# Attention and gMLP on one core: transposes reordered in the first slots, the fifth slot without a group in its first hole, out weights loaded in the ninth slot

## The chip, the cores and the metric

The kernel runs on one core of a Trainium2 chip. The metric is the device time of one execution in microseconds (us), less is better. A core has a matrix engine (TensorE, PE in the profile; PEld is its loading of weights, which overlaps), a vector engine (DVE), a scalar engine (ACT), GpSimd (POOL) and SyncE (SP), which issues all data transfers here. The engines run beside each other, each takes its instructions in order, and semaphores hold an instruction until its inputs are there and its output's buffer is free.

## The reference

Eight batches, eight heads, 576 positions of 64 features. Attention is causal by blocks of 64 positions, and its output goes through a gated feed-forward layer with a product over positions. Cut to what matters:

```python
scores = np.matmul(q, k.transpose(0, 1, 3, 2)) / np.sqrt(D)
scores = np.where(block_i >= block_j, scores, -1e9)
attn = np.exp(scores - np.max(scores, axis=-1, keepdims=True))
attn = attn / (np.sum(attn, axis=-1, keepdims=True) + 1e-09)
x = np.matmul(attn, v)                      # heads side by side: 576 x 512 per batch
h = gelu(x @ w_in)                          # w_in 512 x 1024, tanh form of gelu
u, v = h[..., :512], h[..., 512:]
v_n = (v - mean(v)) / np.sqrt(var(v) + 1e-6) * g_ln
v_s = np.einsum('ts,bsd->btd', w_sg, v_n) + b_sg[None, :, None]
out = x + (u * v_s) @ w_out                 # w_out 512 x 512
```

The weights w_in and w_out arrive as 64-bit floats.

## The kernel before

**Slots.** The work is cut into 32 slots, slot(n) for n from 0 to 31: four pairs of heads for each of eight batches. "The first four slots" are 0 to 3, "the fifth" is slot 4, "the ninth" slot 8. Slot n finishes the attention of pair n (class Values) and makes the scores and exponents of pair n + 1 (class Scores). The names of its tiles are those of the profile:

- pa, pb, pc, pd: transposes of the probabilities. turn0 makes pa (key block 0), one tile per head, turn2 and turn2_rest pb (blocks 2 and 3), turn1 and turn1_rest pc (blocks 1 and 4), turn_first the start of pd. pd and pe later hold the transposed sums as well. Each tile is copied out to pt, for head a by ACT or DVE (table TE). These eight tiles of a slot go through three banks of the accumulator memory, so each waits until the copy of an earlier one, or what else reads it, has left the bank.
- s: the score products. step1 (tiles 4 and 1) and step2 (the rest of tile 4) stand together, step3 (tiles 3 and 0) and step4 (tile 2) later. DVE takes the maxima (negm), ACT the exponents (prob). s and all sums below share five banks.
- ob: attention times v, in av0, av2 and av1. x is the result, multiplied by the transposed reciprocal sums on DVE (x<-pe, x<-pd), and split into xh and xl for the feed-forward.

**Feed-forward of a batch.** It begins in the four slots behind the batch's own: 5 groups of matmuls for v (accv, the first of them the tail of 64 positions), 8 for u (accu), 8 for s (accs, the product over positions), and 8 for the output (acco) one batch later. A group is one step of a generator; hole(k) in a slot takes k groups, and a slot has seven holes, with the counts in PLAN, or in FIRST for slots 4 to 7. The groups of v, u and s of batch 0 lie in slots 4 to 7.

**The side queue.** gelu and the layer norm between v and s are not groups. v_part puts them into a queue, side, when its generator is taken up again behind its fifth group: gelu first (marked "G"), then moments (bs, stats), inverse_std (rs), centre (vv<-vv,stats,g_bc) and scale (vh, vl, vn_t, vone). run_side(k) takes up to k items but stops at a "G"; run_gelu takes a "G" and is called once in a slot, between the sixth and the seventh hole. s_part empties the queue when it begins. The first accs group then needs vh, vl, vn_t and vone.

**Weights.** load_weight loads and splits the weights step by step: from 64 bits (raw) through w to a high part (ACT) and a low part (POOL), with three instructions on DVE, two on ACT and one on POOL for each step, and AHEAD loads in flight. WS has the steps per slot, spread over four places in it; need(part) in the feed-forward takes the steps that are missing.

**Order.** TensorE's instructions keep the order of the program (keep_in_program_order). The order of DVE, ACT, POOL and SP is set when the program is built, by a scheduler that places instructions as they become ready in its model of time; on the chip each engine then runs that list in order. L88 and L91 in the profile are the helpers of matmul and transpose, L101 that of all other engines.

Of the kernel before, what the change touches and what calls it, by code (L numbers as in the profile page):

```python
# [28 lines left out]
def kernel(  # L29
# [13 lines left out]
    B, H, D, S = qT.shape  # L43
    P = 128
    BLK = 64
    DM = H * D
# [22 lines left out]
    def page(dtype, n, name):  # L69
        tag, bufs = KINDS.get(name, KINDS["w"])  # L70
        return sp.tile([P, n], dtype, tag=tag, name=name, bufs=bufs)

    def bank(tag, name, bufs):
        return psum.tile([P, 512], F32, tag=tag, name=name, bufs=bufs)

    def sbank(name):
        return bank("s", name, 5)

    def pbank(name):
        return bank("p", name, 3)  # L80
# [34 lines left out]
    def load_qk(n):  # L115
        b, h = PAIRS[n]
        if n == 0:

            q_f, k_f = page(F32, S, "w"), page(F32, S, "w")
        else:  # L120
            t = sp.tile([P, 2, S], F32, tag="qk_f", name="qk_f", bufs=1)
            q_f, k_f = t[:, 0, :], t[:, 1, :]
        SP.dma_start(q_f, qT[b, h : h + 2].rearrange("a d s -> (a d) s"))
        SP.dma_start(k_f, kT[b, h : h + 2].rearrange("a d s -> (a d) s"))
        qk[n] = (q_f, k_f) if n == 0 else t

    def split_qk(n):
        t = qk[n]
        hi = sp.tile([P, 2, S], F32R, tag="qk_h", name="qk_h", bufs=1)
        lo = sp.tile([P, 2, S], F32R, tag="qk_l", name="qk_l", bufs=1)  # L130
        V.tensor_copy(hi, t)
        for i in (1, 0):
            G.tensor_tensor(lo[:, i, :], t[:, i, :], hi[:, i, :].bitcast(F32), op=ALU.subtract)
        q_h, k_h, q_l, k_l = hi[:, 0, :], hi[:, 1, :], lo[:, 0, :], lo[:, 1, :]
        qk[n] = [(q_h, k_h), (q_h, k_l), (q_l, k_h)]

    def load_v(n):
        b, h = PAIRS[n]
        v_f = v_bufs[n % 2]
        cols = slice(h * D, (h + 2) * D)  # L140
        SP.dma_start(
            v_f[:, : NT - 1, :],
            v[b, : (NT - 1) * P, cols].rearrange("(j p) d -> p j d", p=P),
        )
        SP.dma_start(v_f[:TAIL, NT - 1, :], v[b, S - TAIL :, cols])
        vals[n] = v_f
# [6 lines left out]
    t = sbank("warm")  # L153
# [15 lines left out]
    for s in (0, 1):  # L169
        t = cp.tile([P, NT, 2 * D], F32, name=f"v_f{s}")  # L170
# [5 lines left out]
    for s in range(4):  # L176
        row = []
        for i in range(NT):
            t = cp.tile([P, P * (i + 1) if i else BLK], F32, name=f"prob{s}_{i}")
# [8 lines left out]
    wo_h = cp.tile([P, NC, DM], F32R, name="wo_h")  # L188
    wo_l = cp.tile([P, NC, DM], F32R, name="wo_l")
# [5 lines left out]
    def split_weight(x, dh, dl):  # L195
        A.copy(dh, x)
        G.tensor_tensor(dl, x, dh.bitcast(F32), op=ALU.subtract)

    def from_f64(raw, dh, dl):

        n = raw.shape[-1]
        words = raw.bitcast(U32).rearrange("p (n t) -> p n t", t=2)
        hi, lo = words[:, :, 1], words[:, :, 0]
        tm = page(U32, 2 * n, "w")
        t, m = tm[:, :n], tm[:, n:]

        A.mul(m.bitcast(F32), hi.bitcast(F32), 2.0**-112)

        V.tensor_scalar(t, lo, 29, None, op0=ALU.logical_shift_right)
        V.scalar_tensor_tensor(
            t, hi, 0x80000000, t, op0=ALU.bitwise_and, op1=ALU.bitwise_or
        )
        V.scalar_tensor_tensor(
            t, m, 3, t, op0=ALU.logical_shift_left, op1=ALU.bitwise_or
        )
        split_weight(t.bitcast(F32), dh, dl)

    def load_weight(src, cols, dh, dl):  # L220

        W, AHEAD = 256, 4
        parts = [(c, slice(f, f + W)) for f in range(cols.start, cols.stop, W) for c in range(NC)]
        raws = {}

        def fetch(k):
            if k < len(parts):
                c, fs = parts[k]
                raws[k] = page(src.dtype, W, "raw")
                SP.dma_start(raws[k], src[c * P : (c + 1) * P, fs])  # L230

        for k in range(AHEAD):
            fetch(k)
        for k, (c, fs) in enumerate(parts):
            args = (raws.pop(k), dh[:, c, fs], dl[:, c, fs])
            if src.dtype == F32:
                split_weight(*args)
            else:
                from_f64(*args)
            fetch(k + AHEAD)  # L240
            yield True

    def load_spatial():
        for j in range(NT - 1):
            t = page(F32, S, "w")
            SP.dma_start(t, w_sgT[j * P : (j + 1) * P, :])
            split_weight(t, ws_h[:, j, :], ws_l[:, j, :])
            yield True

        j = NT - 1  # L250
        t = page(F32, S, "w")
        for hf in (0, 1):
            SP.dma_start(t[hf * BLK : (hf + 1) * BLK, :], w_sgT[j * P : S, :])
        t2 = page(F32, S, "w")
        G.memset(t2[BLK:, :], 0.0)
        SP.dma_start(t2[BLK : BLK + 1, :], b_sg.unsqueeze(0))
        SP.dma_start(t2[96:97, :], b_sg.unsqueeze(0))
        A.copy(ws_h[:, j, :], t)
        G.tensor_tensor(
            ws_l[:BLK, j, :], t[:BLK, :], ws_h[:BLK, j, :].bitcast(F32), op=ALU.subtract  # L260
        )
        A.copy(ws_l[BLK:, j, :], t2[BLK:, :])
        V.tensor_tensor(
            ws_l[96:97, j, :], t2[96:97, :], ws_l[96:97, j, :].bitcast(F32), op=ALU.subtract
        )
        yield True

    def load_gains():
# [10 lines left out]
            ("u0", load_weight(w_in, slice(0, DH // 2), wi_h, wi_l)),  # L279
            ("u2", load_weight(w_in, slice(DH // 2, DH), wi_h, wi_l)),  # L280
            ("s", load_spatial()),
            ("o", load_weight(w_out, slice(0, DM), wo_h, wo_l)),
        ]
    )

    def weight_step():

        with ExitStack() as stack:
            for ins in newest.values():
                stack.enter_context(tc.issue_after(ins.ins))  # L290
            while weights and next(weights[0][1], None) is None:
                weights.popleft()
# [96 lines left out]
    class Values:  # L389
# [15 lines left out]
            pt = self.pt[a, j] = sp.tile([P, 512], F32, tag="pt", name="pt", bufs=4)  # L405
            copy(TE[a, j], pt, t)

        def turn0(self, a):

            t = pbank("pa")  # L410
            for i in (4, 3, 2, 1):
                self.turn(a, t[:, (i - 1) * P : i * P], i, 0)
            self.out(a, 0, t)

        def turn2(self):

# [99 lines left out]
    def run_side(k):  # L516

        while k > 0 and side and side[0][0] != "G":
            k -= 1
            side.popleft()[1]()  # L520
# [201 lines left out]
    def hole(k=1):  # L722

        while k > 0 and work:
            try:
                next(work[0])
                k -= 1
            except StopIteration:
                work.popleft()

    WS = [2, 2, 2, 1, 10, 3, 3, 3, 2]

    def load_share(n, k):

        if n < len(WS):
            for _ in range(WS[n] * (k + 1) // 4 - WS[n] * k // 4):
                weight_step()

    PLAN = ["1111111", "1111111", "1111111", "1111112"]

    FIRST = ["1111111", "1111101", "0011011", "1011010"]

    def slot(n, sc):
        va = Values(n, sc)
        nx = Scores(n + 1) if n + 1 < N else None
        g = [int(x) for x in (FIRST if n // 4 == 1 else PLAN)[n % 4]]
        if n + 2 < N:
            load_qk(n + 2)
        if n + 1 < N:
            load_v(n + 1)  # L750
        va.inverse()
        va.turn0(0)
        va.turn0(1)
        hole(g[0])
        load_share(n, 0)
        run_side(2)

        va.turn2()
        va.turn2_rest()
        if nx:  # L760
            nx.step1()
            nx.step2()
        va.av0()
        if nx:
            nx.exponents(1, 4)
        hole(g[1])
        load_share(n, 1)
        run_side(2)
        hole(g[2])
        run_side(2)  # L770
        va.turn1()
        va.turn1_rest()
        va.turn_first()
        if nx:
            nx.step3()
            nx.step4()
        va.av2()
        if nx:
            nx.exponents(3, 0, 2)
        hole(g[3])  # L780
        load_share(n, 2)
        run_side(2)
        va.av1()
        va.av00()
        va.turn_sums()
        hole(g[4])
        va.normalise()

        wait = n // (H // 2) > 0 and n % (H // 2) < 2
        pending.append(va.split)  # L790
        if not wait:
            while pending:
                pending.popleft()()
        run_side(2)
        if n + 2 < N:
            split_qk(n + 2)
        load_share(n, 3)
        hole(g[5])
        run_gelu()
        run_side(3)  # L800
        hole(g[6])
        run_side(3)
        if n % (H // 2) == 1:
            while pending:
                pending.popleft()()
        return nx
# [75 lines left out]
```

## Time and profile before

| | |
|---|---|
| median of 3 runs | 793.02 us (792.67 to 795.04) |
| the profiled execution | 792.86 us, its span 791.0 us |
| instructions | 15794 |
| mean granted clock of TensorE | 0.985 of full speed |
| ACT busy | 450.6 us |
| waits of TensorE for DVE's x, 9 to 62 us | 3.3 us in 3 waits |
| first score products of slots 0 to 4 | 16.38, 31.95, 46.79, 61.62, 82.06 us |
| of slots 5 to 9 | 109.51, 131.27, 151.67, 170.01, 195.54 us |

A row of the timeline has the start and the duration in us, the engine, the helper's line, the operation, output <- inputs with their sizes, and in brackets the idle time of that engine ahead of it with what ended it. A row of the waits has who waited, for whom, the total, how often, and the longest. Windows give the busy time of each engine in a stretch.

### The profile page before, as it was taken

To read this page: it belongs to the slowest core of one execution; us is meant where nothing else is said; L and a number is where in the kernel's file an instruction comes from. 1 tells how busy PE (TensorE), PEld (TensorE's weight loads), DVE (VectorE), ACT (ScalarE), POOL (GpSimd) and SP (SyncE) were. 2 spreads that over 40 slices of the span, in tenths; PEclk is the share of its full clock that TensorE was granted. 3 is DMA by queue.
4 is the path that set the end of the run, shared out by engine and by line. 5 is a ranking of instruction groups with operands and counts; after the bars stand their busy time and mean duration, and the time that the engine had idled before them with its cause. 6 is when DMAs were issued, how large, how long until landed. Compare 5 with 4: busy or idle time off the path is not lost.

```text
span 791.0 us, 15794 instructions
## 1 busy us (share of the span) xinstructions
PE 757.9 (96%) x5926; PEld 640.4 (81%) x5926; DVE 495.5 (63%) x1457; ACT 450.6 (57%) x1172; POOL 272.4 (34%) x331
## 2 busy tenths in 40 slices
PE   7876998999999999999999999999999999999998
PEld 5554786878888888887888888888888978888998
DVE  5888679985866467654866548564676647633532
ACT  4775688567854478435973368544793358721600
POOL 4354265552424124351133414332243510422121
PEclk9989899999999999999999999999999999999999
DMA  7224324212241024311142122410233101320032
GB/s 231 70 92 145 96 91 140 88 61 75 76 150 61 1 76 121 106 60 38 39 136 90 61 75 61 132 65 31 76 107 120 60 7 71 105 76 31 1 120 75
DMA packets 46911, 65.66 MB, mean 83 GB/s; under 512 B 4082, under 2 KB 22514, under 8 KB 46836
## 3 DMA queue, kind: packets, MB, share of 16 engines
q1 hardware_dynamic: 46836, 64.67, 25.5%
q8 instruction: 46, 0.75, 0.4%
q14 instruction: 29, 0.24, 0.1%
HBM read 45.78 MB, written 18.87 MB: 82 GB/s over the span
## 4 chain that ended last, share of the span: by engine, by line
PE 77%; DVE 12%; ACT 8%; issue 1%; SPq 1%; DMA 1%; POOL 1%; DVEq 0%; POOLq 0%; ACTq 0%
PE accs L88 14%; PE acco L88 13%; PE accv L88 13%; PE ob L88 9%; PE s L88 8%; PE accu L88 8%; PE pc L91 3%; PE pb L91 3%; DVE bs L101 3%; ACT prob L101 3%; PE pa L91 2%; DVE w L101 2%; ACT L101 1%; DVE prob L101 1%; PE pe L91 1%; DVE pt L101 1%
## 5 line engine op out<-in xcount | busy, mean ns | idle before, releaser
L101 ACT ACTIVATE prob<-prob,negm 128x448 f32<-128x448 f32 (+4 forms) x320 | 176.3, 554 | 44.1 <-DVE negm L101 41.4
L101 POOL TENSOR_TENSOR qk_l<-qk_f,qk_h 128x576 fp32r<-128x576 f32 x62 | 91.9, 1502 | 231.6 <-issue 98.9
L101 DVE CUSTOM_DVE_ANT_0 prob<-s,mask 128x288 f32<-128x288 f32 (+2 forms) x320 | 117.0, 421 | 64.6 <-PE s L88 64.6
L88 PE MATMUL ob<-pt,v_f 128*64 128x512 f32 (+4 forms) x640 | 105.7, 443 | 0.9 <-ACT pt L101 0.8
L101 POOL TENSOR_TENSOR gl<-u,gh 128x288 fp32r<-128x288 f32 x64 | 51.8, 810 | 108.5 <-DVE gh L101 71.2
L88 PE MATMUL s<-qk_h 64*128 64x288 f32 (+1 forms) x372 | 87.4, 341 | 0.4 <-ACT u L101 0.4
L88 PE MATMUL accu<-xh,wi_h 128*128 128x288 f32 x256 | 78.1, 305 | 5.1 <-DVE negm L101 5.1
L88 PE MATMUL s<-qk_l,qk_h 64*128 64x288 f32 (+1 forms) x372 | 82.2, 302 | 0.0
L88 PE MATMUL accs<-ws_h,vh 128*128 128x288 f32 x256 | 78.2, 305 | 1.5 <-DVE negm L101 1.5
L88 PE MATMUL s<-qk_h,qk_l 64*128 64x288 f32 (+1 forms) x372 | 77.9, 299 | 0.0
L88 PE MATMUL acco<-gh,wo_h 128*128 128x288 f32 x256 | 77.7, 303 | 0.0
L88 PE MATMUL accs<-ws_h,vl 128*128 128x288 f32 x256 | 75.6, 295 | 0.0
L88 PE MATMUL accs<-ws_l,vh 128*128 128x288 f32 x256 | 75.5, 295 | 0.0
L88 PE MATMUL accu<-xl,wi_h 128*128 128x288 f32 x256 | 75.5, 295 | 0.0
L88 PE MATMUL accu<-xh,wi_l 128*128 128x288 f32 x256 | 75.4, 295 | 0.0
L88 PE MATMUL acco<-gl,wo_h 128*128 128x288 f32 x256 | 75.4, 294 | 0.0
L88 PE MATMUL acco<-gh,wo_l 128*128 128x288 f32 x256 | 75.4, 294 | 0.0
L88 PEld LDWEIGHTS ob<-pt,v_f 128*64 128x64 f32 x640 | 38.2, 137 | 42.0 <-issue 29.4
L88 PE MATMUL accv<-wi_h,xh 128*128 128x512 f32 x160 | 66.0, 413 | 3.8 <-POOL xh L101 3.8
L88 PEld LDWEIGHTS s<-qk_h 64*128 64x128 f32 x372 | 64.0, 188 | 1.4 <-ACT u L101 0.6
L101 DVE TENSOR_TENSOR u<-accs,u 128x288 f32<-128x288 f32 x64 | 29.2, 456 | 55.4 <-PE accs L88 55.3
L88 PEld LDWEIGHTS s<-qk_h,qk_l 64*128 64x128 f32 x372 | 63.8, 187 | 0.0
(104 smaller groups left out, 1954.6 us busy)
## 6 DMA issues: line engine op xcount, KB each, us to landing
spill<-x SPq DMA_DIRECT2D x32, 288.0 KB, 3.8
xr<-spill SPq DMA_DIRECT2D x32, 288.0 KB, 3.3
out_T<-xr SPq DMA_DIRECT2D x32, 288.0 KB, 3.3
qk_f<-in_qT SPq DMA_DIRECT2D x31, 288.0 KB, 3.2
qk_f<-in_kT SPq DMA_DIRECT2D x31, 288.0 KB, 3.8
v_f<-in_v SPq DMA_DIRECT2D x32, 256.0 KB, 3.1
raw<-in_w_in SPq DMA_DIRECT2D x16, 256.0 KB, 4.8
raw<-in_w_out SPq DMA_DIRECT2D x8, 256.0 KB, 4.8
```

The costliest lines, as they stand in the source:

```text
L88: return pin(nc.tensor.matmul(*a, **k), "P")
L91: return pin(nc.tensor.transpose(out, in_, identity), "P")
L101: return lambda *a, **k: pin(f(*a, **k), self.letter)
```

## The change

Four things change. turn0 makes the transposes of both heads together, tiles 4, 3 and 1 of each head first and tile 2 of both last; this holds in all slots. In slots 0 to 3 the products step1 and step2 and av0 stand right behind turn0, and turn2 and turn2_rest follow av0. FIRST has no group in the first hole of slot 4, and one in the sixth hole of slot 5 that had none; so slot 4 has six groups and slot 5 seven. The weight steps of slots 4 to 8 are 8, 5, 0, 0, 8 instead of 10, 3, 3, 3, 2, and the out weights have 2 loads in flight instead of 4.

```diff
--- before.py
+++ after.py
@@ -217,9 +217,9 @@
         )
         split_weight(t.bitcast(F32), dh, dl)
 
-    def load_weight(src, cols, dh, dl):
-
-        W, AHEAD = 256, 4
+    def load_weight(src, cols, dh, dl, AHEAD=4):
+
+        W = 256
         parts = [(c, slice(f, f + W)) for f in range(cols.start, cols.stop, W) for c in range(NC)]
         raws = {}
 
@@ -279,7 +279,7 @@
             ("u0", load_weight(w_in, slice(0, DH // 2), wi_h, wi_l)),
             ("u2", load_weight(w_in, slice(DH // 2, DH), wi_h, wi_l)),
             ("s", load_spatial()),
-            ("o", load_weight(w_out, slice(0, DM), wo_h, wo_l)),
+            ("o", load_weight(w_out, slice(0, DM), wo_h, wo_l, 2)),
         ]
     )
 
@@ -405,12 +405,15 @@
             pt = self.pt[a, j] = sp.tile([P, 512], F32, tag="pt", name="pt", bufs=4)
             copy(TE[a, j], pt, t)
 
-        def turn0(self, a):
-
-            t = pbank("pa")
-            for i in (4, 3, 2, 1):
-                self.turn(a, t[:, (i - 1) * P : i * P], i, 0)
-            self.out(a, 0, t)
+        def turn0(self):
+
+            t = [pbank("pa"), pbank("pa")]
+            for tiles in ((4, 3, 1), (2,)):
+                for a in (0, 1):
+                    for i in tiles:
+                        self.turn(a, t[a][:, (i - 1) * P : i * P], i, 0)
+            for a in (0, 1):
+                self.out(a, 0, t[a])
 
         def turn2(self):
 
@@ -728,7 +731,7 @@
             except StopIteration:
                 work.popleft()
 
-    WS = [2, 2, 2, 1, 10, 3, 3, 3, 2]
+    WS = [2, 2, 2, 1, 8, 5, 0, 0, 8]
 
     def load_share(n, k):
 
@@ -738,7 +741,7 @@
 
     PLAN = ["1111111", "1111111", "1111111", "1111112"]
 
-    FIRST = ["1111111", "1111101", "0011011", "1011010"]
+    FIRST = ["0111111", "1111111", "0011011", "1011010"]
 
     def slot(n, sc):
         va = Values(n, sc)
@@ -749,18 +752,22 @@
         if n + 1 < N:
             load_v(n + 1)
         va.inverse()
-        va.turn0(0)
-        va.turn0(1)
+        va.turn0()
         hole(g[0])
         load_share(n, 0)
         run_side(2)
 
-        va.turn2()
-        va.turn2_rest()
+        early = n < H // 2
+        if not early:
+            va.turn2()
+            va.turn2_rest()
         if nx:
             nx.step1()
             nx.step2()
         va.av0()
+        if early:
+            va.turn2()
+            va.turn2_rest()
         if nx:
             nx.exponents(1, 4)
         hole(g[1])
```

**TensorE, slot 0.** These are rows of the difference of the two orders, from the last transposes of block 0 (pa, both heads) to the products of step 1; prob_3 is tile 3 of the probabilities, x2 stands for one row per head.

```order
 L91 MATMUL pa<-ident,prob_3_123 128x128
+L91 MATMUL pa<-ident,prob_1_119 128x128
+L91 MATMUL pa<-ident,prob_2_112 128x128
 L91 MATMUL pa<-ident,prob_2_121 128x128
-L91 MATMUL pa<-ident,prob_1_119 128x128
+L88 MATMUL s<-qk_h 128x288 x2
+L88 MATMUL s<-qk_l,qk_h 128x288 x2
```

The transposes of tile 1 move ahead of those of tile 2, and the products of step 1, which stood behind the ten transposes of pb, now stand ahead of them, with step 2 and av0 behind.

**ACT, slot 1, after the change.** From the exponents of tiles 1 and 4 of the next pair to the copies of pc (w is the weight step, pt the copies):

```order
L101 ACTIVATE prob2_1_128,sums_599<-prob2_1_128,negm_601 128x192
L101 ACTIVATE prob3_1_137,sums_599<-prob3_1_137,negm_602 128x192
L101 ACTIVATE prob2_4_134,sums_599<-prob2_4_134,negm_601 128x576
L101 ACTIVATE prob3_4_143,sums_599<-prob3_4_143,negm_602 128x576
L101 ACTIVATE w_678<-raw_321 128x256
L101 COPY pt_668<-pb_658 128x512
L101 COPY pt_695<-pc_685 128x512
L101 COPY pt_699<-pc_686 128x512
```

Before, the copy of pb stood ahead of the first of these exponents; now it stands behind the last and behind w.

**DVE, the layer norm of batch 0, before the change.** Between the x of slot 4's pair and the first maxima that follow it (bs and stats are the moments, vv the centring):

```order
L101 BN_STATS bs<-vv 128x6 [waits Activation_49]
L101 COPY pt<-pa 128x512 [waits PE_49]
L101 SCALAR_TENSOR_TENSOR vv<-vv,stats,g_bc 128x512 x2
L101 BN_AGGR stats<-bs 128x2 [waits DVE_49]
L101 BN_STATS bs<-vv 64x6 [waits Activation_49]
L101 COPY pt<-pb 128x512 [waits PE_49]
L101 BN_AGGR stats<-bs 64x2 [waits DVE_49]
```

After the change the same work stands one slot later, behind the casts xh of the last two pairs, the first of which waits for TensorE:

```order
L101 CAST xh<-x 128x576 [waits PE_49]
L101 CAST xh<-x 128x576 [waits DVE_49,PE_49]
L101 TENSOR_TENSOR ws_l<-w,ws_l 1x576 [waits DMAHW5_49,Activation_49]
L101 BN_STATS bs<-vv 128x6
L101 COPY pt<-pa 128x512 [waits PE_49]
L101 BN_AGGR stats<-bs 128x2 [waits DVE_49]
L101 BN_STATS bs<-vv 128x6
L101 SCALAR_TENSOR_TENSOR vv<-vv,stats,g_bc 128x512 [waits DVE_49]
```

and its end, the scaling, directly ahead of the first result of accs:

```order
L101 SCALAR_TENSOR_TENSOR vv<-vv,stats,g_bc 64x512
L101 SCALAR_TENSOR_TENSOR vn_t<-vv,rs,vn_t 64x512 [waits Activation_49]
L101 SCALAR_TENSOR_TENSOR vl<-vv,rs,vh 128x512 [waits Activation_49] x2
L101 SCALAR_TENSOR_TENSOR vl<-vv,rs,vh 128x512 [waits DVE_49,Activation_49] x2
L101 TENSOR_TENSOR u<-accs,u 128x288 [waits PE_49]
```

Before, the vl of batch 0 stood ahead of slot 6's maxima, between x and the copies of pa and pb. The first accs group has the same place on TensorE in both: right behind av0 of slot 6.

## The prediction

> **What bounds the kernel now.** I read the busy times first, then TensorE's waits, then the busy times by stage, and last the timeline at the places where the waits stand. A stage here is one slot, from the first score product of a slot to that of the next.
>
> ```profile
> PE 757.9 (96%) x5926; PEld 640.4 (81%) x5926; DVE 495.5 (63%) x1457; ACT 450.6 (57%) x1172; POOL 272.4 (34%) x331
> ```
>
> TensorE is busy for 757.9 of 791.0 us, so 33 us of idle time are all that an order of work can win, and whatever makes TensorE wait anew is paid in full. The waits of TensorE between 60 and 160 us (who waits, for whom, total, times, longest):
>
> ```profile
> PE accv L88 <- POOL xh L101: 3.8, 1, 3.8
> PE pa L91 <- ACT pt L101: 2.1, 1, 2.1
> ...
> PE accu L88 <- DVE negm L101: 0.7, 1, 0.7
> ...
> PE s L88 <- ACT u L101: 0.4, 1, 0.4
> ```
>
> And all of its waits behind 160 us:
>
> ```profile
> PE accu L88 <- DVE negm L101: 4.3, 6, 0.7
> ```
>
> So 630 of the 791 us have 4.3 us of waits in them; a gain or a loss is made ahead of 160 us, or the change makes a wait in the steady part. The windows by stage (window and its length; busy time with the number of instructions for PE, PEld, DVE, ACT, POOL; granted clock; DMA share; GB/s), for slots 3 to 4, 4 to 5, 5 to 6 and 8 to 9:
>
> ```profile
> 61.62:82.06 20.44, 14.48 (x105) 10.15 (x104) 14.93 (x45) 11.34 (x34) 9.42 (x11) 0.84 0.44 139
> 82.06:109.51 27.45, 27.44 (x182) 21.82 (x181) 18.26 (x55) 20.96 (x53) 12.48 (x12) 0.93 0.34 111
> 109.51:131.27 21.76, 18.43 (x158) 14.97 (x157) 18.92 (x48) 18.08 (x43) 11.45 (x11) 1.00 0.28 90
> 170.01:195.54 25.53, 25.53 (x181) 20.61 (x180) 15.73 (x49) 18.05 (x47) 6.64 (x8) 1.00 0.18 60
> ```
>
> Ahead of 82 us no engine is full: a chain bounds (maxima on DVE, exponents on ACT, transposes on PE, x on DVE). From there on TensorE bounds. That decides how the parts below are priced: in slots 0 to 3 by the chain, later by what TensorE waits for.
>
> **The change, part by part. First, slots 0 to 3.** The rows of slot 1, of one answer of the timeline (start, duration, engine):
>
> ```profile
> 32.80 0.59 ACT L101 COPY pt<-pb 128x512 f32<-128x512 f32 x1 [2.22 <-PE pb L91]
> 33.87 0.46 DVE L101 CUSTOM_DVE_ANT_0 prob<-s,mask 128x288 f32<-128x288 f32 x1 [0.52 <-PE s L88]
> 36.64 0.44 PE L88 MATMUL s<-qk_h 64*128 64x448 f32 x1
> 37.28 0.42 ACT L101 ACTIVATE w<-raw 128x256 f32<-128x256 f32 x1
> 37.73 0.42 DVE L101 SCALAR_TENSOR_TENSOR w<-w 128x256 uint32<-128x256 uint32 x1 [0.92 <-ACT w L101]
> 38.07 0.62 DVE L101 CUSTOM_DVE_ANT_0 prob<-s,mask 128x448 f32<-128x448 f32 x1
> ```
>
> The products of step 1 no longer stand behind ten pb transposes but behind five pa transposes, so the first maximum (33.87) comes some 0.5 us sooner. But the eight transposed tiles of a slot share three banks, and the banks of pc and pd are now those that pb has only just filled: ACT's copy of pb, before at 32.80, stands behind the exponents of tiles 1 and 4 and behind w in ACT's order. It can begin at 37.28 + 0.42 = 37.7, which is 3.8 us behind the first maximum, ends at 4.4, and only then come pd, and the products of step 3 (before 36.64, 2.8 behind the first maximum) at 4.6. The third maximum follows 1.1 us later, 5.7 behind the first one instead of 38.07 - 33.87 = 4.2. Net of the 0.5 us: 1.0 us later in slot 1. In slot 2 the first and third maximum of before stand 53.62 - 48.71 = 4.9 apart:
>
> ```profile
> 48.71 0.46 DVE L101 CUSTOM_DVE_ANT_0 prob<-s,mask 128x288 f32<-128x288 f32 x1 [0.52 <-PE s L88]
> ...
> 53.62 0.62 DVE L101 CUSTOM_DVE_ANT_0 prob<-s,mask 128x448 f32<-128x448 f32 x1 [0.64 <-PE s L88]
> ```
>
> So the same working gives 5.7 - 4.9 - 0.5 = 0.3 us there, and I take 0.5; as much in slot 3, where no w stands in ACT's order and the distance of before is that of slot 1. In slot 0 ACT's copy of pb stands behind the cast of wi_h too, which waits for DVE, and I take 2.0 us. Sum of the slip: **4.0 us**, between 2.5 and 6.
>
> What this does to slot 4, from its rows:
>
> ```profile
> 67.83 0.62 DVE L101 CUSTOM_DVE_ANT_0 prob<-s,mask 128x448 f32<-128x448 f32 x1 [2.21 <-PE s L88]
> ...
> 74.69 0.40 PE L88 MATMUL accv<-wi_h,xh 128*128 128x512 f32 x1
> ...
> 74.92 0.40 PE L88 MATMUL accv<-wi_l,xh 128*128 128x512 f32 x1
> ...
> 76.95 0.21 DVE L101 TENSOR_TENSOR x<-pd,x 128x64 f32<-128x64 f32 x1
> ...
> 79.62 0.80 PE L88 MATMUL accv<-wi_h,xh 128*128 128x512 f32 x1 [3.83 <-POOL xh L101]
> ...
> 80.64 1.78 PE L91 MATMUL pb<-ident,prob 128*128 128x128 f32 x7
> 82.06 0.61 PE L88 MATMUL s<-qk_h 64*128 64x288 f32 x1
> ```
>
> Without a group in its first hole, pb waits only for x to leave its bank (76.95 + 0.21 = 77.16), and products follow 82.06 - 80.64 = 1.42 us later: 78.6 instead of 82.06, 3.5 us sooner. One weight step less on DVE ahead of it gives 0.6 more. Against it stands the slip of 4.0. Products of slot 4 so begin at 82.0: **term 0**, between -1.5 and +2.5. The 3.83 and 2.13 us of waits are gone, but they were cover for the group that stood between them, the tail group of v: eight matmuls at a pitch of 74.92 - 74.69 = 0.23 us, **+1.85 us**, now have to be done where TensorE is full.
>
> **Second, the moments of batch 0.** This is the largest term. The empty hole moves the fifth group of v from the fifth hole to the sixth. The code that queues gelu, moments, centring and scaling runs when v's generator is taken up again, at the hole after. That was the sixth hole, just ahead of the slot's one call of run_gelu; it is now the seventh, behind it. The gelu stands first in the side queue and blocks it until the next call, one slot later. In the order of DVE the moments so move from slots 4/5 to behind the last u group (the casts xh, which overwrite what that group reads), and the maxima of slot 6 and all vl stand between them and the first accs group; that group has kept its place on TensorE. What each costs, on DVE unless said:
>
> ```profile
> 106.69 0.66 DVE L101 BATCH_NORM_STATS2 bs<-vv 128x6 f32<-128x512 f32 x1
> ...
> 107.48 0.66 DVE L101 BATCH_NORM_STATS2 bs<-vv 128x6 f32<-128x512 f32 x1
> ...
> 111.44 0.67 DVE L101 COPY pt<-pb 128x512 f32<-128x512 f32 x1
> ...
> 112.11 0.42 DVE L101 CUSTOM_DVE_ANT_0 prob<-s,mask 128x288 f32<-128x288 f32 x1
> ...
> 114.27 2.07 DVE L101 SCALAR_TENSOR_TENSOR vv<-vv,stats,g_bc 128x512 f32<-128x512 f32 x3
> ```
> ```profile
> 116.96 0.72 ACT L101 ACTIVATE vn_t<-vv,rs 64x512 fp32r<-64x512 f32 x1
> 117.58 0.71 ACT L101 ACTIVATE vone<-vv,rs 64x512 fp32r<-64x512 f32 x1
> ```
> ```profile
> 125.42 1.84 DVE L101 SCALAR_TENSOR_TENSOR vl<-vv,rs,vh 128x512 fp32r<-128x512 f32 x1
> ...
> 128.57 0.82 DVE L101 CAST xh<-x 128x576 fp32r<-128x576 f32 x2
> 129.31 0.81 DVE L101 SCALAR_TENSOR_TENSOR vl<-vv,rs,vh 128x512 fp32r<-128x512 f32 x1
> 130.04 0.68 DVE L101 COPY pt<-pa 128x512 f32<-128x512 f32 x1
> ```
> ```profile
> 126.71 0.29 PE L88 MATMUL accu<-xl,wi_h 128*128 128x288 f32 x1
> 126.84 0.29 PE L88 MATMUL accu<-xh,wi_l 128*128 128x288 f32 x1
> ...
> 135.12 0.40 PE L88 MATMUL accs<-ws_h,vh 128*128 128x288 f32 x1 [0.68 <-DVE negm L101]
> ```
>
> Let T be the end of the last u group, 126.84 + 0.29 = 127.1 here. Behind T, DVE does xh twice (0.75), one row of ws_l (0.7, an estimate from a copy of that length), five moments with their aggregates (107.48 - 106.69 = 0.79 each, 3.95), two copies (1.3), six maxima (114.27 - 112.11 = 2.15), three weight instructions (about 0.4 each, 1.1) and five centrings (2.07 / 3 each, 3.45): 13.4 us. ACT then needs vn_t, vone and the first vh, at 117.58 - 116.96 = 0.62 of pitch and 0.72 for the first, 1.95; DVE four vl at 130.04 - 129.31 = 0.73, 2.9; and the group ends 0.6 later: T + 18.9. Before, the group began at 135.12 and, at 126.84 - 126.71 = 0.13 us for each of 14 matmuls of the same size, ended at 137.0 = T + 9.9. The difference is 9.0; DVE will also wait once for the products, which stand behind copies that stand between the moments, and I add 0.5: **+9.5 us**. The lower end is 5.7: three moments and two centrings ahead of the first maximum (3.8) would then fill time in which DVE waits for products anyhow. The upper end is 12, with vl nearer to the 1.84 us of the row at 125.42 than to 0.81.
>
> In slot 5 DVE loses this work, and the 0.7 and 0.4 us of waits shown above for accu and s go: **-1.1 us**.
>
> **Third, the clock.** After a long wait the matmuls run at half clock; window of 4 us, its length, PE busy, granted clock, DMA:
>
> ```profile
> 82.00:86.00 4.00, 4.00 (x27) 0.52 0.63 243
> ```
>
> This stands behind the 3.83 us wait. A new idle stretch of about 10 us in slot 6, where the clock was 1.00, should bring such a stretch behind it: 4 us at half clock are 2 us of work lost, **+2 us**, between 0 and 3.4. [...]
>
> **Fourth, the out weights.** Seven of the eight steps now fall into the ninth slot, where one or two were. A step is three DVE instructions at about 0.4, two on ACT at about 0.4 and one on POOL: some 6 us more on DVE and 5 on ACT, in a slot of 25.53 us with 15.73 and 18.05 busy. It fits on both, and TensorE's work hides it; with a depth of two loads instead of four and DVE's order fuller, a copy can come late. Between 0 and 3, I take **+0.5**. Slots 6 and 7 lose the steps, which costs and wins nothing where TensorE bounds.
>
> **Sum.** 0 + 1.85 + 9.5 - 1.1 + 2 + 0.5 = +12.75 us. The profiled run took 792.86 us (791.0 of span and 1.9 around it), 0.16 below the median of the runs; so 805.6, and **806** beside the median.
>
> **Rivals.**
> - *Faster.* The earlier products win in every slot, the bank does not bind, and the moments find gaps. Then four slots gain 0.5 each, slot 4 gains 3.5 + 0.6, slot 5 gains 1.1, the group costs 1.85: -5.4, **788**. For it: TensorE waits 3.83 and 2.13 us in slot 4 of before, and those waits do go. Against it: ACT and DVE take their work in order, and vl cannot run ahead of the moments. It decides from accs in slot 6 waiting under 5 us. Chance 0.05.
> - *Half the price.* The moments fill DVE's waits (5.7), no clock loss, slip 2.5: -1.5 + 1.85 + 5.7 - 1.1 = +5, **798**. Chance 0.15.
> - *A second new bound, the ninth slot.* The main case and, beside it, out weights that delay copies, +3, or a slip at its upper end, +2.5: **811**. Chance 0.2.
> - *It washes out.* The LN wait comes at its lower end and the waits removed pay for it: within 2.4 us of before. Chance 0.04.
> - The main case, 802 to 809: 0.56.
>
> **Numbers.** Range 797 to 815: from the half price less 1 to all upper ends (2.5 + 1.85 + 12 - 1.1 + 3.4 + 3 = +21.7). A difference of 0.3% is 2.4 us, about what a measurement of this kernel can tell from none. Faster 0.05, within it 0.04, slower 0.91.
>
> **What would show it.** The moments right behind the casts of xh at the end of slot 5; a wait of accs for DVE or ACT of some 9 to 11 us in slot 6; a granted clock near 0.5 behind it; no wait of accv for xh; products of slot 4 within 2.5 us of 82; and a third maximum 5 us or more behind the first in slots 1 to 3. From slot 9 on the pitch of four slots stays. I am wrong if accs of slot 6 waits under 5 us, or if products of slot 4 begin under 79.

## The result, and the profile after

| | before | changed |
|---|---|---|
| median of 4 runs | 793.35 us (792.67 to 795.04) | 810.78 us (810.04 to 813.97) |
| the profiled execution | 792.86 us, span 791.0 | 813.97 us, span 812.1 |
| mean granted clock of TensorE | 0.985 | 0.968 |
| score products of slots 4, 6, 7 and 9 begin | 82.06, 131.27, 151.67, 195.54 us | 87.04, 138.64, 168.87, 215.96 us |

The changed kernel is slower: ratio 1.0229, 95% interval 1.0202 to 1.0255, or 17.4 us between the medians. Its profiled execution is the longest of its four runs, 3.2 us above their median, so differences of the two profiles add up to 21 us, not 17; the experiments below are compared by their medians.

The windows by stage of the changed kernel (window and length, then busy time of PE, PEld, DVE, ACT, POOL, granted clock, DMA share, GB/s), for slots 2 to 3, 3 to 4, 4 to 5, 5 to 6, 6 to 7 and 8 to 9:

```profile
50.74:67.53 16.79, 12.87 (x96) 8.75 (x95) 12.36 (x38) 10.08 (x32) 7.55 (x10) 0.80 0.39 130
67.53:87.04 19.51, 14.39 (x104) 10.04 (x103) 13.59 (x40) 10.69 (x32) 7.96 (x10) 0.76 0.32 101
87.04:114.05 27.01, 27.01 (x178) 21.66 (x177) 13.51 (x50) 18.89 (x50) 11.46 (x11) 0.95 0.36 117
114.05:138.64 24.59, 19.92 (x169) 16.71 (x168) 15.36 (x38) 20.21 (x48) 15.20 (x14) 0.98 0.35 107
138.64:168.87 30.23, 22.37 (x168) 19.20 (x167) 22.08 (x62) 14.90 (x36) 11.18 (x13) 0.79 0.12 40
187.30:215.96 28.66, 25.91 (x182) 20.61 (x181) 21.12 (x59) 19.91 (x52) 8.67 (x11) 1.00 0.30 93
```

Three places lose. Slot 4 begins 5.0 us later than before (87.04 against 82.06). Between slots 4 and 7 it takes 168.87 - 87.04 = 81.8 us instead of 69.6, 12.2 more. The stage of slot 8 takes 28.66 us instead of 25.53, 3.1 more. That is 20.3 of the 21.1 us between the two spans; slot 9, with 22.40 us instead of 21.70, has most of the rest. The waits of TensorE, first up to 160 us, then between 180 and 217 us:

```profile
PE pa L91 <- DVE x L101: 15.0, 4, 4.8
PE accs L88 <- ACT vh L101: 7.7, 1, 7.7
PE pb L91 <- DVE pt L101: 4.6, 1, 4.6
...
PE pc L91 <- ACT pt L101: 1.9, 1, 1.9
```
```profile
PE pb L91 <- ACT pt L101: 1.7, 1, 1.7
PE pa L91 <- DVE x L101: 1.1, 1, 1.1
PE ob L88 <- DVE vv L101: 0.7, 1, 0.7
PE accv L88 <- DVE negm L101: 0.4, 1, 0.4
```

The wait of accv for xh, 3.8 us before, is gone, and so are those of accu and s in slot 5. New is that of accs for vh, and that of pb for pt has grown from 1.9 to 4.6 us, both in slot 6; in the early slots pa now waits for x. The place in slot 6, in rows of the timelines of the four engines:

```profile
131.67 0.29 PE L88 MATMUL accu<-xh,wi_l 128*128 128x288 f32 x1
```
```profile
132.36 3.30 DVE L101 CAST xh<-x 128x576 fp32r<-128x576 f32 x1
```
```profile
129.31 4.38 POOL L101 TENSOR_TENSOR ws_l<-w,ws_h 128x576 fp32r<-128x576 f32 x3
133.66 0.31 POOL L101 TENSOR_TENSOR xh<-x,xh 128x64 fp32r<-128x64 f32 x1
133.94 1.41 POOL L101 TENSOR_TENSOR xl<-x,xh 128x576 fp32r<-128x576 f32 x1
```
```profile
136.46 0.69 DVE L101 BATCH_NORM_STATS2 bs<-vv 128x6 f32<-128x512 f32 x1
...
146.85 0.74 DVE L101 SCALAR_TENSOR_TENSOR vv<-vv,stats,g_bc 64x512 f32<-64x512 f32 x1
```
```profile
148.03 0.72 ACT L101 ACTIVATE vn_t<-vv,rs 64x512 fp32r<-64x512 f32 x1 [0.66 <-POOL rs L101]
```
```profile
150.03 0.61 PE L88 MATMUL accs<-ws_h,vh 128*128 128x288 f32 x1 [7.68 <-ACT vh L101]
...
154.15 1.07 PE L91 MATMUL pc<-ident,prob 128*128 128x128 f32 x6
```

The moments begin right behind the casts of xh, the last centring at 146.85, vh follows on ACT, and TensorE gets its accs group only then. With T = 131.67 + 0.29 = 132.0 the group ends at 154.15 = T + 22.2. It runs at half clock, as the windows of 4 us show (length, PE busy, clock, DMA):

```profile
146.00:150.00 4.00, 0.00 (x0) 0.50 0.00 0
150.00:154.00 4.00, 3.79 (x14) 0.50 0.00 0
```

### The profile page after: what moved, and what is told of

Read it like the earlier page. It is cut to its first block, busy times and chain, and to the rows that moved or that the text cites. A ratio compares the mean times of both kernels' runs of the same rounds, so it can differ in the third digit from the quotient of the medians.

```text
span 812.1 us, 15781 instructions
## 1 busy us (share of the span) xinstructions
PE 766.6 (94%) x5926; PEld 646.6 (80%) x5926; DVE 494.8 (61%) x1457; ACT 453.0 (56%) x1172; POOL 273.3 (34%) x331
## 4 chain that ended last, share of the span: by engine, by line
PE 81%; DVE 12%; ACT 4%; issue 1%; DMA 1%; POOL 0%; SPq 0%; DVEq 0%; ACTq 0%
PE accs L88 15%; PE acco L88 13%; PE accv L88 12%; PE ob L88 10%; PE accu L88 9%; PE s L88 9%; PE pc L91 4%; PE pb L91 3%; PE pa L91 3%; DVE w L101 2%; DVE bs L101 2%; DVE prob L101 2%; PE pe L91 1%; DVE pt L101 1%; DVE vv L101 1%
## 5 line engine op out<-in xcount | busy, mean ns | idle before, releaser
L101 ACT ACTIVATE prob<-prob,negm 128x448 f32<-128x448 f32 (+4 forms) x320 | 176.3, 553 | 45.6 <-DVE negm L101 42.9
L101 POOL TENSOR_TENSOR qk_l<-qk_f,qk_h 128x576 fp32r<-128x576 f32 x62 | 94.2, 1539 | 244.2 <-issue 109.7
L88 PE MATMUL ob<-pt,v_f 128*64 128x512 f32 (+4 forms) x640 | 107.5, 451 | 0.7 <-DVE vv L101 0.7
L101 ACT COPY pt<-pa 128x512 f32<-128x512 f32 x32 | 18.6, 581 | 85.2 <-PE pa L91 85.2
```

Of the source, the lines that this page charges most:

```text
L88: return pin(nc.tensor.matmul(*a, **k), "P")
L101: return lambda *a, **k: pin(f(*a, **k), self.letter)
```

## The experiments

Where a difference is shown against the changed kernel, the rest of that kernel stands; where against before, likewise. Every run was timed beside runs of the kernel before on the same chip.

**1. The side queue, mended in the changed kernel.**

```diff
         hole(g[6])
+        if n == H // 2:
+            run_gelu()
         run_side(3)
```

> The changed kernel with one more call of run_gelu in slot 4, behind its last hole, so that the layer norm of batch 0 is queued in slot 4 again. Theory A (the blocked side queue is the largest cost): the wait of accs for vh in slot 6 (7.7 us) and the longer wait of pb for pt ahead of it go, the time falls by 9 to 12 us, to about 801. Rival B (the slower first slots and the clock are the cost, the norm would have been waited for anyway): within 3 us of the changed kernel's 811.

Measured: 804.74 us, 6.0 less than the changed kernel; ratio to before 1.0148 (1.0115 to 1.0182). The wait for vh went, so the queue was blocked as the prediction said, but 6.0 is short of the 9 to 12 expected. The stages of slots 5 and 6 show the rest:

```profile
113.07:133.35 20.28, 19.57 (x169) 16.52 (x168) 16.38 (x46) 18.71 (x46) 11.95 (x11) 1.00 0.34 94
133.35:159.69 26.34, 21.95 (x168) 18.49 (x167) 18.83 (x49) 15.20 (x38) 14.32 (x17) 0.87 0.18 64
```

Slot 5 is mended (20.28 us, 24.59 in the changed kernel), slot 6 is still 5.9 us above the 20.40 of before. The longest wait of TensorE in it is that of accs for DVE's maxima:

```profile
PE accs L88 <- DVE negm L101: 2.5, 1, 2.5
```

Ahead of these maxima, on DVE and on POOL, stand:

```profile
135.42 3.34 DVE L101 TENSOR_TENSOR ws_l<-w,ws_l 1x576 fp32r<-1x576 f32 x1 [0.89 <-ACT ws_l L101]
```
```profile
133.44 1.42 POOL L101 TENSOR_TENSOR ws_l<-w,ws_h 64x576 fp32r<-64x576 f32 x1
...
136.74 1.40 POOL L101 TENSOR_TENSOR xl<-x,xh 128x576 fp32r<-128x576 f32 x1
```

One row of 576 elements takes DVE 3.34 us, 1.36 before. It ends at 138.76, 0.6 us after POOL's unbroken run of subtractions (136.74 + 1.40). In the changed kernel the cast of 3.30 us ended at 135.66, 0.3 us after POOL's run (133.94 + 1.41). That gave the next theory: the spatial weights, five steps in slot 5 instead of three, put POOL's work where DVE's is due.

**2. FIRST and the weight steps alone, without the new order of transposes and products.** FIRST by itself was not tried.

```diff
-    WS = [2, 2, 2, 1, 10, 3, 3, 3, 2]
+    WS = [2, 2, 2, 1, 8, 5, 0, 0, 8]
-    FIRST = ["1111111", "1111101", "0011011", "1011010"]
+    FIRST = ["0111111", "1111111", "0011011", "1011010"]
```

> The kernel before with the new FIRST and the new weight steps (8, 5, 0, 0, 8, two loads ahead), with the transposes and products in the old order. Theory A: +10 for the side queue, +1.9 for the tail group, -4 for the waits of slot 4 that go, +0 to 3 for the ninth slot: 801 to 805. Rival B: the empty first hole only wins, 788 to 794.

Measured: 805.68 us, ratio 1.0153 (1.0115 to 1.0192), just above the 805 of theory A; rival B falls. So 12 us of the 17 come without any new order in the first slots. Products of slot 4 begin at 77.97 us there, 4.1 sooner than before, which is the gain that the empty hole was worth (3.5 in the prediction); all but 0.7 of it is lost again when the products of slot 6 begin (130.55 us, 131.27 before).

**3. The new order of transposes and products alone** (turn0 and the early products, with the old FIRST, steps and loads ahead).

> The kernel before with the new order of transposes and products alone (turn0 in all slots, products ahead of pb in slots 0 to 3), with the old FIRST and weight steps. Theory A: the first slots slip by the 8 us that the changed kernel's profile shows at the third maximum of slot 3 (76.03 against 67.83), nothing is won back in slot 4: about 801, 799 to 803. Rival C (the slip of 4 us of the prediction, the rest comes of the other edits): 795 to 798.

Measured: 798.74 us, ratio 1.0071 (1.0046 to 1.0096): 5.2 us, just below the 799 of theory A and above rival C. Slot 4 begins at 89.67 us in its profile, 7.6 later than before; 1.7 of it comes back in the next stage (25.75 us against 27.45), where TensorE is full. Experiments 2 and 3 add up to the whole loss: 12.2 + 5.2 = 17.4 us.

**4. The weight steps alone** (WS and two loads ahead, on the kernel before).

> The kernel before with the new weight steps and two loads ahead for the out weights alone. Theory A: the waits of slot 8 that the changed kernel's profile shows (1.1 + 0.7 + 0.4 + 1.7 us, the stage 3.1 us longer) come with it, 795 to 797. Rival D (those waits come of the shifted order behind the layer norm, not of the out weights): within 1.5 us of before.

Measured: 797.30 us, ratio 1.0054 (1.0037 to 1.0070), 0.3 us above the range of theory A. Its stage of slot 8 is as long as that of the changed kernel, with the same waits, and rival D falls:

```profile
170.79:199.56 28.77, 25.92 (x182) 20.61 (x181) 21.24 (x59) 19.91 (x52) 8.77 (x11) 1.00 0.30 94
```

**5. turn0 alone**, on the kernel before.

> The kernel before with the new turn0 alone (both heads' first tiles together, tile 2 last, in all slots); products stay behind pb. Theory E (of the early slots' cost a part is turn0 itself: five transposes of pa now wait for x to leave its bank, where before only pb did): first products of slots 1 to 4 come 0.5 to 1 us later each, 795 to 797. Rival F (only the products ahead of pb cost): within 1.2 us of before.

Measured: 794.52 us, ratio 1.0011 (0.9999 to 1.0022). By the time it is rival F (1.2 us), by the profile theory E: products of slots 1 to 4 begin at 32.42, 48.97, 64.97 and 86.17 us, up to 4.1 us later than before, and pa waits for x instead of pb:

```profile
PE pa L91 <- DVE x L101: 17.3, 5, 5.7
```

Its stage of slot 4 is then 1.7 us shorter (25.74 against 27.45). Some 2.3 us of the loss stay to the end of this profile (span 793.3 us against 791.0), while the medians differ by 1.2; so the time alone would have hidden the mechanism.

**6. Filler transposes in the changed kernel**, to keep TensorE at work while it waits for x in slots 1 to 4. They repeat the transposes of head a into their own bank.

```diff
                 for a in (0, 1):
+                    if a == 1 and tiles[0] == 4 and 0 < self.n <= H // 2:
+                        for _ in range(8):
+                            for i in tiles:
+                                self.turn(0, t[0][:, (i - 1) * P : i * P], i, 0)
                     for i in tiles:
```

> The changed kernel with 24 more transposes in each of slots 1 to 4, repeats of those of head a into their own bank, in the time in which TensorE waits for x; the results stay the same. Theory G (half clock behind that wait is a good part of the slip in slots 1 to 4): granted clock near 1.0 in these stages, 2 to 4 us less than the changed kernel's 810.8. Rival H (the order of the copies of pb and pc is the slip): clock up, time within 1.5 us of 810.8.

Measured: 806.36 us, 4.4 less than the changed kernel with more work for TensorE. The stages of slots 1, 2 and 3:

```profile
34.62:49.07 14.45, 12.78 (x120) 9.74 (x119) 12.64 (x39) 10.00 (x31) 6.90 (x8) 1.00 0.31 94
49.07:63.47 14.40, 12.80 (x121) 9.77 (x121) 12.32 (x39) 10.01 (x32) 7.57 (x9) 1.00 0.44 139
63.47:80.24 16.77, 14.02 (x128) 10.45 (x127) 13.68 (x41) 10.71 (x32) 7.79 (x10) 0.96 0.38 116
```

The clock is 1.00 instead of 0.80 in slot 2, and slots 1 to 3 take 45.6 us instead of 52.5. Theory G holds, with a gain 0.4 us above its range. Rival H falls: the time moved by more than its 1.5 us, and up to the end of slot 3, ACT, DVE and POOL run the same instructions in the same order in both runs, but for two neighbours swapped on ACT. How much of the slip half clock made is not shown, because the kernel before has half clock in these slots too. Slots 1 to 3 together, in the kernel before, in experiment 2 (the same FIRST and weights, the old order) and in the changed kernel:

```profile
31.95:82.06 50.11, 38.43 (x295) 26.95 (x294) 39.59 (x120) 31.11 (x96) 23.70 (x28) 0.84 0.38 118
31.86:77.97 46.11, 36.16 (x288) 25.66 (x287) 38.26 (x117) 29.68 (x93) 21.48 (x25) 0.83 0.34 106
34.57:87.04 52.47, 39.44 (x294) 26.85 (x293) 38.80 (x117) 30.95 (x94) 22.62 (x27) 0.80 0.32 104
```

Against experiment 2 the new order costs 6.4 us in these slots, and the filler takes 6.9 off. But it takes off nearly all half clock (1.00, 1.00 and 0.96), that of the old order too, and no run put it into the kernel before. In windows of 1 us from 10 to 90 us, of the kernel before and of the changed one, the clock is 0.50 or 1.00, with values between only where it passes from one to the other. Taken so for experiment 2 as well, the means 0.83 and 0.80 stand for 15.7 us and 21.0 us at half clock, and the 5.3 us more for at most 2.7 us of lost work; that is an estimate from these rows.

In the changed kernel these windows show 0.50 behind the wait of 2.8 us for x in slot 1 (36 to 38 us) and around the end of those of 3.7, 3.6 and 4.8 us in slots 2 to 4 and behind it (49 to 55, 66 to 72 and 83 to 89 us). In the kernel before 0.50 also stands from 32 to 34 us, behind waits of 1.5 and 1.0 us with 0.7 us of work between them, so a stretch with some work in it was enough here.

**7. The old order, the new FIRST with the call of run_gelu, the old weight steps** (with two loads ahead).

> The kernel before with the new FIRST and the additional call of run_gelu in slot 4, with the old weight steps and two loads ahead. Theory A: slot 4 starts 4.1 us sooner as in the run with FIRST and the weight steps, the tail group costs 1.9, slot 5 loses its waits of about 1: 788 to 791. Rival (the rest of the loss in slot 6 belongs to the later group of v, not to the weights): 793 to 798.

Measured: 795.04 us, ratio 1.0015 (1.0002 to 1.0028). The time is that of the rival. Slot 4 begins at 75.54 us, 6.5 sooner than before, and slot 5 takes 25.5 us instead of 21.8, in a profile that is 1.7 us under the median. (Slots 0 to 3 are the same program in experiments 2, 7 and 9, and slot 4 begins at 77.97, 75.54 and 78.16 us, so single profiles differ by some 2.6 us there.) A long row of ws_l stands on DVE again, and TensorE waits behind it:

```profile
122.61 3.48 DVE L101 TENSOR_TENSOR ws_l<-w,ws_l 1x576 fp32r<-1x576 f32 x1
```
```profile
128.55 1.20 PE L91 MATMUL pb<-ident,prob 128*128 128x128 f32 x4 [5.42 <-DVE pt L101]
```

So the reason given for the rival (the later group of v) was not the one that showed; experiment 9 decides.

**8. Where the out weights cost.** Weight steps 8, 5, 3, 3, 2 and two loads ahead, on the kernel before.

> The kernel before with weight steps 8, 5, 3, 3, 2 and two loads ahead: two of the spatial weights' steps in slot 5 instead of slot 4, the out weights nearly where they were. Theory I (the out weights in the ninth slot cost the 3.2 us of that stage, the spatial ones in slot 5 about 1.5 us in slot 6): 794 to 795.5, the ninth stage 25.5 us as before. Rival J (two loads ahead or the shift of all weights costs it): the ninth stage stays near 28.7, 796 to 798.

Measured: 796.01 us, ratio 1.0032 (1.0021 to 1.0043); neither theory as stated. The stage of slot 8:

```profile
172.17:199.01 26.84, 25.68 (x181) 20.59 (x180) 14.46 (x47) 17.15 (x44) 5.67 (x7) 1.00 0.18 62
```

26.84 us lies between 25.53 and 28.77: two loads ahead cost 1.3 us with the steps nearly where they were (a weight step then stands ahead of the sum vv of v's tail in DVE's order, and ob waits for vv, 0.8 us in experiment 9, which has the same steps there), the eight steps in one slot 1.9 more. Experiments 9 and 12, which differ in the loads ahead alone, have the same 1.3 us there (26.84 and 25.55).

**9. All spatial weights in slot 4**, in the kernel of experiment 7.

```diff
-    WS = [2, 2, 2, 1, 10, 3, 3, 3, 2]
+    WS = [2, 2, 2, 1, 13, 0, 3, 3, 2]
```

> As the run with the old order, new FIRST and the call of run_gelu (795.0 us), but with all five steps of the spatial weights in slot 4 (13, 0, 3, 3, 2). Theory K (POOL's ws_l beside DVE's xh and ws_l at the end of slot 5 holds DVE up for 3 us and more): the stage from slot 5 to 6 falls from 25.5 to 21 to 22 us, total 790 to 792. Rival L (DVE has too much of its own there): the stage stays above 24, total 794 to 796.

Measured: 788.46 us, ratio 0.9944 (0.9930 to 0.9959), below both kernels. Slots 5 and 6 of it:

```profile
106.10:127.04 20.94, 19.57 (x169) 16.52 (x168) 17.27 (x49) 17.79 (x44) 7.72 (x9) 1.00 0.27 75
127.04:146.04 19.00, 19.00 (x167) 16.26 (x167) 16.21 (x50) 13.79 (x38) 11.78 (x14) 1.00 0.34 113
```

Rival L falls by its own numbers; theory K named the right place, with a total 1.5 us too high. The stages are even 0.8 and 1.4 us shorter than before the change (21.76 and 20.40).

**10. The same in the changed kernel with the call of run_gelu** (13, 0, 0, 0, 8).

> The changed kernel with the call of run_gelu in slot 4 and all spatial weights in slot 4 (13, 0, 0, 0, 8). Theory K: no DVE instruction of over 2 us at the end of slot 5, slot 6 back to about 21 us from 26.3, total 799 to 801 against 804.7 without the move. Rival L: 803 to 805.

Measured: 799.24 us, 5.5 less than experiment 1, as theory K said, and no DVE instruction takes over 2 us. Slot 6, which took 26.34 us there, is now:

```profile
134.32:153.77 19.45, 19.07 (x168) 16.26 (x167) 13.85 (x45) 12.44 (x34) 11.27 (x14) 1.00 0.19 65
```

Not all of the 5.5 us need come of long DVE instructions. In experiment 4 the spatial weights stand in slot 5 too and no DVE instruction takes over 2 us, yet slot 6 is 1.5 us longer than before (21.94 against 20.40), and accs waits for the weights themselves:

```profile
PE accs L88 <- DVE ws_l L101: 1.1, 1, 1.1
```

**11. All mendings in the changed kernel**: call of run_gelu, filler, spatial weights in slot 4, out weights in slots 6 to 8 with three loads ahead.

> The changed kernel with all mendings: the filler transposes, the call of run_gelu, the spatial weights in slot 4 and the out weights in slots 6 to 8 with three loads ahead. If the named costs add up: 810.8 - 4.4 (clock) - 6 (side queue) - 4 (spatial weights) - 2.5 (ninth slot) = 793 to 795. If they overlap, or something else was in the change: 797 or more.

Measured: 788.65 us, ratio 0.9949 (0.9934 to 0.9964): 22 us less than the changed kernel and 5 less than the sum of the costs named until then. The four together make up for more than the whole loss. Most of the surplus lies in two terms that the sum had too small: the spatial weights, 5.5 us in experiment 10 instead of 4, and the out weights, 4.7 instead of 2.5 (against experiment 10, slots 7 and 8 take 17.15 and 25.55 us instead of 18.42 and 28.99).

**12. Three loads ahead**, in the kernel of experiment 9.

> As the run with the old order, new FIRST, the call of run_gelu and all spatial weights in slot 4 (788.5 us), with three loads ahead for the out weights instead of two. Theory M (with two loads ahead the out weights' steps fall in the way of the tail's sum in slot 8, as its wait of ob for vv shows): stages 7 and 8 fall from 18.3 and 26.8 to 17.2 and 25.5 us as in the run with all mendings, total 785.5 to 787. Rival N (those stages were shorter there for the new turn0): 788 to 789.

Measured: 786.40 us (785.67 to 786.84), ratio 0.9916 (0.9903 to 0.9930), the fastest kernel here. Slots 7 and 8 of it, with TensorE without a gap:

```profile
146.09:163.24 17.15, 17.15 (x147) 14.10 (x147) 13.10 (x44) 9.50 (x29) 11.86 (x14) 1.00 0.26 88
163.24:188.79 25.55, 25.55 (x181) 20.52 (x180) 17.14 (x50) 18.59 (x48) 7.15 (x9) 1.00 0.23 75
```

These are theory M's stages, with the old turn0, so rival N falls. Against the kernel before it differs in four things: no group in the first hole of slot 4 (and one more in slot 5), one more call of run_gelu in that slot, the spatial weights in slot 4, and three loads ahead instead of four. Experiment 11 has these four as well, with the new order and the filler, and takes 2.3 us more. Its products of slot 4 begin 2.7 us later (81.56 us against 78.85), and all of that is there at slot 1 already (34.59 against 31.86): the filler leaves out slot 0, and the cost of the new order there stays.

## Why the prediction was right, and where not

The direction, the main mechanism and the range held: 806 forecast, 810.8 measured, inside 797 to 815. The main case, 802 to 809, was missed.

- **The side queue** (+9.5, +2 for the clock, -1.1, +1.85 for the tail group: 12.25 us between slots 4 and 7). The two profiles differ by 12.2 us there, and most signs named were seen: the moments behind the casts of xh, accs waiting, the clock at 0.50 behind it, no wait of accv for xh, a third maximum over 5 us behind the first. Two were not: accs waited 7.7 us instead of 9 to 11, and slot 4 began 5.0 us late. The wait itself is split in two, 4.6 for pt and 7.7 for vh; of these the prediction had only the second, of 9 to 11. The sum was right partly by luck: undoing the blocked queue won 6.0 us, and moving the spatial weights another 5.5. The prediction counted the row of ws_l at 0.7 us and the casts of xh at 0.75, and did not ask what POOL would be doing beside them; the two casts took 4.84 us together. The group ended at T + 22.2, not T + 18.9. The clock term was too small as well: 0.50 stands around the end of the first wait and behind it, from 137.6 to 141.0 us, and in the second and behind it, from 144.4 to 154.7, where TensorE worked 3.2 + 4.5 = 7.7 us, so it is nearer to 4 us than to 2, an estimate. No run shows the 3.4 us that stand as the upper end of this term; in their place the windows show 7.7 us of work at 0.50.
- **Slot 4's start** (term 0, the slip of 4.0 us): this step failed. The third maximum of slot 3 came 8.2 us later (67.83 before), and slot 4 5.0 later, twice the upper end that was given. Against experiment 2, which has the old order with the same FIRST and weights, slot 4 begins 9.1 us later (87.04 against 77.97). That is the slip (7.6 by experiment 3 against the kernel before), forecast at 4.0 and at most 6: slot 0 has 2.7 of it (forecast 2.0), slots 1 to 3 have 6.4 (forecast 2.0). The row of the maximum, and that of slot 4's wait:

```profile
76.03 0.62 DVE L101 CUSTOM_DVE_ANT_0 prob<-s,mask 128x448 f32<-128x448 f32 x1 [1.79 <-PE s L88]
```
```profile
84.40 1.33 PE L91 MATMUL pa<-ident,prob 128*128 128x128 f32 x5 [4.82 <-DVE x L101]
```

  The reordering was read rightly: in slot 1 the third maximum stood 42.24 - 35.77 = 6.5 us behind the first, where 5.7 was worked out and 4.2 was before; with the filler, at full clock, it is 41.11 - 35.63 = 5.5.

```profile
35.77 0.46 DVE L101 CUSTOM_DVE_ANT_0 prob<-s,mask 128x288 f32<-128x288 f32 x1 [0.35 <-PE s L88]
...
42.24 0.62 DVE L101 CUSTOM_DVE_ANT_0 prob<-s,mask 128x448 f32<-128x448 f32 x1 [1.46 <-PE s L88]
```

  What was missed is how long TensorE waits for x (15.0 us in slots 1 to 4) and at what clock it goes on. Five transposes of pa now stand behind x in each of these slots, ahead of pb; by experiment 5 the new turn0 alone begins slot 4 4.1 us later. The prediction priced every transpose and product of these slots as before, where the mean clock is 0.84, and asked for more half clock only in slot 6; it fell to 0.80. Experiment 6, with the clock at 1.00, 1.00 and 0.96, wins back as much as slots 1 to 3 lost (6.9 us of 6.4). How that loss is shared between the waits and the added half clock stays open.
- **The ninth slot** (+0.5, 0 to 3): mis-sized. The stage grew by 3.1 us. It does fit on DVE and ACT, as argued, but order decided, not room: a weight step ahead of the tail's sum on DVE, and on ACT a weight cast ahead of the copy of v's last group (vv). That group was done at 207.79, the cast waited for DVE until 209.44, and the gelu, the copy of pa and the transposes of pb that need its bank all come behind it. Experiments 8 and 12 split the loss into loads ahead and steps.

```profile
209.44 0.41 ACT L101 CAST wo_h<-w 128x256 fp32r<-128x256 f32 x1 [2.20 <-DVE w L101]
209.75 0.58 ACT L101 COPY vv<-accv 128x512 f32<-128x512 f32 x1
```

- **The gain of slot 4** (3.5, and 0.6 for a weight step less) was right: 4.1 in experiment 2.
- **The rivals.** "A second new bound, the ninth slot", with a slip at its upper end, 811, came closest to the time, and both of its parts happened. The faster rival's condition, accs waiting under 5 us, was not met; once the blocked queue and the weights are mended its time, 788, is about what comes (786.4 to 788.7).

## What to carry to other kernels

When work is moved by one place, ask what is triggered by position: here an empty hole made a generator run out one hole later, past the only call that empties a queue, and a whole layer norm went into the critical path. Where an order makes TensorE wait longer, read the granted clock behind that wait before pricing what follows, and test the price with harmless filler work on the waiting engine, in the kernel before as well. A change with four parts can hide a gain: alone, the empty hole with its queue and weights put right is worth 0.8%.

## What the runs showed of the hardware that was not expected

Three DVE instructions took 3.3 to 3.5 us beside an unbroken run of POOL's subtractions: the cast of xh (3.30 us in the changed kernel; 0.45 to 1.03 in the 32 casts of the kernel before), and the single row of ws_l (3.34 and 3.48 in experiments 1 and 7; 1.36 before). Each ended 0.3 to 0.6 us after that run of POOL. But the cast just ahead of the first one ended while the run went on, 0.3 us after one subtraction of it had ended:

```profile
130.82 1.62 DVE L101 CAST xh<-x 128x576 fp32r<-128x576 f32 x1 [2.70 <-PE accu L88]
```
```profile
130.70 1.43 POOL L101 TENSOR_TENSOR ws_l<-w,ws_h 128x576 fp32r<-128x576 f32 x1
```

What decides when such an instruction ends is therefore open. The runs moved the work apart, and the long instructions went with it (the two casts, 4.84 us together in the changed kernel, take 0.82 in experiments 9 and 10); none changed POOL's work alone, so the cause in the hardware is not shown.

Twenty-four transposes in each of slots 1 to 4, whose results are not needed, made the changed kernel 4.4 us faster: the granted clock of slots 1 to 3 rose from 0.84, 0.80 and 0.76 to 1.00, 1.00 and 0.96.
